# Chunk states of a state-space layer stored 576 instead of 512 bytes apart in SBUF

## The chip, the cores and the metric

The kernel runs on one core of a Trainium2 chip. The metric is device time in microseconds, the median of several executions.

## The reference, cut to what matters

Two branches are computed from the same `x` (2048 x 512) and mixed by a gate. One is softmax attention with 32 heads of 16 channels, the other a diagonal state-space convolution over 2048 steps with 512 channels.

```python
def _A_ref(x, wqkv, wo):                       # attention: 32 heads, Dh = 16
    scores = jnp.einsum("bhqd,bhkd->bhqk", q, k) * Dh ** -0.5
    p = _softmax(scores, axis=-1)              # 32 x 2048 x 2048 exponentials
    ...
def _B_ref(u, A_re, A_im, ...):                # state space, 128 states per channel
    K = jnp.einsum("dn,dnl,dn->dl", Cc, P, dB).real
    y = irfft(rfft(u) * rfft(K))               # causal convolution along time
    ...
return g * a + (1 - g) * b
```

The kernel computes the convolution in chunks of 64 steps. For each channel, a chunk leaves a complex state of 128 numbers (one per partition). A scan on VectorE carries the states from chunk to chunk, and the output of a chunk is a local product plus the carried state times a table.

Of the kernel before, what the change touches and what calls it, by code (L numbers as in the profile page):

```python
# [17 lines left out]
NCH = S // T  # L18
NBLK = 16
CB = D // NBLK  # L20
HALF_PI = math.pi / 2
NDSEM = 56

# [221 lines left out]
def declare(nc, es):  # L245
    B = {}

    def sb(name, free, dt=BF16):
        B[name] = Buf(name, "sb", free, dt)


    sb("KT", 4 * S)
    for k in range(4):
        sb(f"Q{k}", 4 * 512)
    sb("Qm", 2 * 512)
    sb("VE", 16 * 560)
    sb("ET", 7 * 1024)
    for k in range(4):
        sb(f"OnT{k}", S)
    sb("OT", 512, FP32)  # L260
    sb("ON", 512)
    sb("Rz", 2 * 16, FP32)
    sb("Wo", 4 * D)
    sb("xT", 4 * S)
    for n in ("Wk", "Wq", "Wv"):
        sb(n, 4 * D)
    sb("msk", 2, FP32)
    sb("piota", 4, FP32)
    sb("hpi", 1, FP32)

    sb("gwT", 4)
    sb("wm", D)
    sb("x0n", 4 * D)
    sb("idf", P, FP32)
    sb("idb", P)
    sb("gp", 16, FP32)
    sb("ge", 16, FP32)
    sb("g", 16, FP32)
    sb("g1", 16, FP32)
    sb("Dpb", 16)  # L280
    sb("Dp", 16, FP32)
    sb("Yl", 16 * D)
    sb("fo", 4 * D)

    for n in ("AreT", "AimT", "BreT", "BimT", "CreT", "CimT", "ldt", "dt"):
        sb(n, D)
    for n in ("an", "bn", "ba", "ea", "e2", "sb_", "cb", "u1", "u2", "u3", "u4", "zr", "zi"):
        sb(n, D, FP32)
    sb("wrb", D)
    sb("nwi", D)  # L290
    sb("VV", 2 * D, FP32)
    sb("VL", 2 * D, FP32)
    for n in ("L1", "L2", "L4", "L8", "L16", "L32", "L48"):
        sb(n, 2 * D, FP32)
    sb("MU", 3 * D, FP32)
    sb("pt1", 2 * D, FP32)
    sb("pt2", 2 * D, FP32)
    for n in ("D16", "D32", "D48"):
        sb(n, 2 * 2 * D)

    sb("FP", 2 * 128 * 8, FP32)
    sb("ft1", 2 * 64 * 8, FP32)
    sb("ft2", 2 * 64 * 8, FP32)
    for k in range(4):
        sb(f"B16{k}", 2 * 128 * 16)

    sb("PT", 2 * 2 * CB * T)
    sb("tt1", 2 * CB * 16)
    sb("tt2", 2 * CB * 16)
    sb("Qt", 2 * 32 * 128)  # L310
    sb("Sst", 4 * 512)
    sb("Kst", 2 * 8 * P)

    sb("SG0", 33 * 2 * 128)
    sb("SG1", 33 * 2 * 128)
    sb("G", 2 * 128, FP32)
    for n in ("s2", "s3"):
        sb(n, 2 * 128, FP32)

    sb("X2", 4 * 32 * 64)  # L320

    sb("Py", 3 * 2 * 16 * T)
    sb("Tt", 3 * 8 * 64)
    sb("Yst", 2 * 256)
    for i in range(3):
        B[f"SC{i}"] = Buf(f"SC{i}", "ps", 1024, FP32)
    B["OA"] = Buf("OA", "ps", 512, FP32)
    B["MB"] = Buf("MB", "ps", 512, FP32)
    for n, free in (("ptd", NBLK * P * 2 * CB * T), ("sd", D * NCH * 2 * P),
                    ("kpd", NBLK * P * 8 * P), ("xrd", S * D), ("ytd", D * S)):  # L330
        B[n] = Buf(n, "dr", free, BF16)
        B[n].t = nc.dram_tensor("gm_" + n, [free // P, P], BF16)
    for n in ("SC0", "SC1", "SC2", "OA", "MB"):
        B[n].t = es.enter_context(nc.psum_tensor(n, [P, B[n].free], FP32))
    for n in ("x", "w", "wo", "are", "aim", "bre", "bim", "cre", "cim", "ldt_d", "dsk_d", "gw_d", "out"):
        B["d_" + n] = Buf("d_" + n, "dr", 1, BF16)
    return B


def place(nc, bufs):  # L340

    base, end = (nc.sbuf_base + 31) // 32 * 32, nc.sbuf_usable_end
    sbs = [b for b in bufs.values() if b.kind == "sb" and b.first is not None]

    def fit(order):
        done, top = [], base
        for b in order:
            n = (b.nbytes() + 31) // 32 * 32
            busy = sorted((o.lo, o.hi) for o in done if o.first <= b.last + 1 and b.first <= o.last + 1)
            at = base  # L350
            for lo, hi in busy:
                if at + n <= lo:
                    break
                at = max(at, hi)
            b.lo, b.hi = at, at + n
            top = max(top, b.hi)
            done.append(b)
        return top

    best, seed = None, 1  # L360
    for k in range(400):
        def rank(b):
            nonlocal seed
            seed = (seed * 1103515245 + 12345) % 2 ** 31
            w = seed / 2 ** 31 * (0 if k < 2 else .8)
            return (-(b.last - b.first > 300) if k % 2 else 0, -b.nbytes() * (1 + w * 2) * (b.last - b.first + 20) ** (w if k >= 2 else 0))
        order = sorted(sbs, key=rank)
        top = fit(order)
        if best is None or top < best[0]:
            best = (top, order)  # L370
    assert best[0] <= end, (best[0] - end, live(sbs))
    fit(best[1])
    for b in sbs:
        b.over = [o for o in sbs if o is not b and o.lo < b.hi and b.lo < o.hi]
        b.order = b.first
        b.t = nc.alloc_sbuf_tensor_at(b.name, [P, b.free], b.dt, offset=b.lo)
    for b in bufs.values():
        if b.kind != "sb":
            b.over, b.order = (), 0
# [27 lines left out]
def record(nc, p, B, ins):  # L407
# [426 lines left out]
    def sload(blk):  # L834
        qr, bl = divmod(blk, 4)
        yield ("AFTER", f"S{blk}", 2)
        if qr >= 2:
            yield ("AFTER", f"yq{qr - 2}", 0)
        sg = SG[qr % 2]
        if bl == 0:  # L840
            op("POOL", lambda g: g.memset(sg(0, [[1, 256]]), 0.0), [], [(sg, "z")])
        dma("SP", lambda e: e.dma_start_transpose(sg(256 + CB * bl, [[128, 64], [1, CB]]),
                                                  sd.dram(CB * blk * 8192, [[8192, CB], [1, 8192]])),
            [(sd, (blk, i)) for i in range(4)], [(sg, bl, (qr, 'S'))])
        sch.mark(f"sg{blk}")


    def scan():
        G, s2, s3 = B["G"], B["s2"], B["s3"]
        MU = B["MU"]  # L850
        e = "DVE"

        def quarter(qr):
            sg, d0 = SG[qr % 2], 128 * qr
            ks = [(sg, bl, (qr, 'S')) for bl in range(4)]
            for bl in range(4):
                yield ("AFTER", f"sg{4 * qr + bl}", 12)
            for c in range(NCH - 1):
                so = 256 * (c + 1)
                if c == 0:  # L860
                    yield (e, .3)
                    op(e, lambda v, so=so: v.tensor_copy(G(0, [[1, 256]]), sg(so, [[1, 256]])), ks, [(G, 0)])
                    continue
                yield (e, .7)
                op(e, lambda v: v.tensor_tensor(s2(0, [[128, 2], [1, 128]]), G(0, [[128, 2], [1, 128]]),  # L865
                                                MU(d0, [[0, 2], [1, 128]]), ALU.mult), key("G", "MU"), [(s2, 0)])
                op(e, lambda v: v.tensor_tensor(s3(0, [[128, 2], [1, 128]]), G(128, [[-128, 2], [1, 128]]),  # L867
                                                MU(D + d0, [[D, 2], [1, 128]]), ALU.mult), key("G", "MU") + [(MU, 1)], [(s3, 0)])
                yield (e, .9)
                op(e, lambda v, so=so: v.tensor_tensor(s2(0, [[1, 256]]), s2(0, [[1, 256]]), sg(so, [[1, 256]]), ALU.add),  # L870
                   [(s2, 0)] + ks, [(s2, 0)])
                op(e, lambda v: v.tensor_tensor(G(0, [[1, 256]]), s2(0, [[1, 256]]), s3(0, [[1, 256]]), ALU.add),  # L872
                   [(s2, 0), (s3, 0)], [(G, 0)])
                op(e, lambda v, so=so: v.tensor_copy(sg(so, [[1, 256]]), G(0, [[1, 256]])), key("G"), ks)  # L874
            for bl in range(4):
                sg.tags[bl] = (qr, "G")
            sch.mark(f"scan{qr}")

        yield ("AFTER", "scanpar", 0)
        for qr in range(4):  # L880
            yield from quarter(qr)
# [20 lines left out]
    def ystage():  # L902
        def unit(u):
# [11 lines left out]
            for q in range(4):  # L915
# [7 lines left out]
                for ri in range(2):  # L923
                    for j in range(4):
                        i = 4 * q + j
                        mm(lambda q=q, j=j: MB(64 * q, [[1, 64]], 32 * j, 32),
                           lambda ri=ri, i=i: sg(ri * 128 + CB * bl + 16 * hf + i, [[256, 32]]),
                           lambda ri=ri, i=i: Py(r * YN + ri * 16 * T + i * T, [[1, T]]),
                           [(sg, b_, (qr, 'G')) for b_ in range(4)] + [(sg, "z"), (Py, r, u)], ky, False, ri == 1,
                           pos=(0, 32 * j))  # L930
# [241 lines left out]
```

## The kernel before: what the change touches

`SG0` and `SG1` hold the states of one quarter of the channels (128 channels), each in turn. A row of `SG` has 128 real parts, then 128 imaginary parts, as bf16. So the states of one channel in successive chunks lie 2 x 128 elements = 512 bytes apart.

```python
sb("SG0", 33 * 2 * 128)                 # 32 chunks and one row of zeros
sb("SG1", 33 * 2 * 128)
...
def sload(blk):                         # 16 blocks of 32 channels
    ...
    dma("SP", lambda e: e.dma_start_transpose(sg(256 + CB * bl, [[128, 64], [1, CB]]), ...
def quarter(qr):                        # the scan, on VectorE
    for c in range(NCH - 1):
        so = 256 * (c + 1)
        ...                             # s2 = G * MU_re ; s3 = swap(G) * MU_im
        op(e, lambda v, so=so: v.tensor_tensor(s2(0, [[1, 256]]), s2(0, [[1, 256]]), sg(so, [[1, 256]]), ALU.add), ...
        ...                             # G = s2 + s3
        op(e, lambda v, so=so: v.tensor_copy(sg(so, [[1, 256]]), G(0, [[1, 256]])), ...
def ystage():                           # the output: 32 units of 4 steps; one step is
    ...                                 # 4 matmuls MB<-Tt,X and these 8 matmuls MB<-Py,SG
        mm(lambda q=q, j=j: MB(64 * q, [[1, 64]], 32 * j, 32),
           lambda ri=ri, i=i: sg(ri * 128 + CB * bl + 16 * hf + i, [[256, 32]]),   # weights
           lambda ri=ri, i=i: Py(r * YN + ri * 16 * T + i * T, [[1, T]]), ...
```

The weights of such a matmul are 32 columns (one channel, 32 chunks), read with a step of 256 elements. `X`, the weight operand of the matmuls `MB<-Tt,X` and `MB<-Qt,X`, is read with a step of 64 elements (128 bytes).

Everything is recorded by a small scheduler in steps of one key tile `q` (0 to 511). In each step ScalarE runs two exponentials of 128x1024, TensorE runs the attention matmuls `SC<-Qm,KT` and `OA<-ET,VE`, and pieces of the state-space work are dealt out by a budget. All state-space matmuls write one PSUM tile, `MB`, so a piece must be evicted by VectorE before the next may start (in the kernel before, the matmuls `MB<-Qt,X` waited 22.1 us for this and `MB<-Tt,X` 8.4 us).

The softmax here doesn't subtract the row's maximum and nothing guards it: scores larger than these inputs give would overflow.

## Time and profile before

| what | value | where it is read |
|---|---|---|
| time | 1044.11 us (4 runs) | results |
| ScalarE busy | 978.2 us, 94% | page, part 1 |
| of it exponentials | 963.9 us in 1024 | page, part 5 |
| spacing of exponentials, undisturbed | 904 ns | records of the trace |
| the same beside `Py,SG` matmuls | 1078 ns | records of the trace |

In the views PE is TensorE's matmuls, PEld its weight loads, DVE is VectorE, ACT is ScalarE and POOL is GpSimd. The granted clock is the share of its full speed that TensorE was given. The page's first lines for the kernel before, with the busy time of each engine:

```profile
span 1040.5 us, 16316 instructions
...
PE 752.9 (72%) x6617; PEld 212.2 (20%) x6617; DVE 636.2 (61%) x1356; ACT 978.2 (94%) x1041; POOL 3.5 (0%) x11
```

ScalarE is the limit. At the undisturbed spacing its 1024 exponentials take 1023 x 0.904 = 925 us from the first start to the last. Where the rest goes is seen in the windows view of the kernel before. The columns are the stretch, then busy time and number of instructions on each engine, the granted TensorE clock, the DMA share and GB/s.

```profile
100.00:150.00 50.00, 36.68 (x266) 9.13 (x265) 41.19 (x58) 49.86 (x55) 0.00 (x0) 0.91 0.00 1
650.00:700.00 50.00, 42.63 (x484) 16.70 (x480) 6.39 (x14) 49.05 (x51) 0.31 (x1) 0.50 0.51 112
800.00:850.00 50.00, 41.80 (x480) 16.66 (x476) 43.41 (x113) 48.94 (x50) 0.00 (x0) 0.50 0.41 96
850.00:900.00 50.00, 43.90 (x496) 17.05 (x492) 4.31 (x11) 50.00 (x51) 0.00 (x0) 0.50 0.34 83
```

Read the fourth engine, ACT: from 850 to 900 us it is busy all of the time, but finishes 51 exponentials where it finished 55 in the earlier stretch. It is not waiting; each instruction takes longer. By the records, an exponential beside a `Py,SG` burst took 1256 ns (median) and the others of the output stage 1114 ns. In that stretch the output is computed. The timeline of the kernel before shows two of its steps (start, duration, engine, line, what, how many; idle time in brackets):

```profile
859.84 0.61 PE L420 MATMUL SC<-Qm,KT 32*128 32x512 bf16 x4 [0.18 <-ACT ET L537]
...
860.93 0.15 PEld L420 LDWEIGHTS MB<-Tt,X 64*32 64x32 bf16 x4 [0.44 <-issue]
860.93 0.28 PE L420 MATMUL MB<-Tt,X 64*32 64x64 bf16 x4
861.14 0.34 PEld L420 LDWEIGHTS MB<-Py,SG 128*32 128x32 bf16 x8
861.15 0.47 PE L420 MATMUL MB<-Py,SG 128*32 128x64 bf16 x8
861.79 0.11 PEld L420 LDWEIGHTS SC<-Qm,KT 32*128 32x128 bf16 x4 [0.31 <-ACT ET L537]
861.80 0.61 PE L420 MATMUL SC<-Qm,KT 32*128 32x512 bf16 x4 [0.18 <-ACT ET L537]
```

From one `SC` group to the next is 1.96 us for two exponentials. TensorE waits for ScalarE there (0.18 us), so TensorE is not the limit. The eight `Py,SG` weight loads take 0.34 us together.

The durations by tile in the kernel before (minimum, median, maximum in ns) compare the weight loads, and show a VectorE operation of the scan:

```profile
L420 PEld LDWEIGHTS MB<-Py,SG x1024: 162/226/279, 619.1 to 907.1; 128*32 128x32 bf16 x171
L420 PEld LDWEIGHTS MB<-Qt,X x512: 128/144/169, 247.7 to 617.5; 64*32 64x32 bf16 x171
L420 PEld LDWEIGHTS MB<-Tt,X x512: 128/137/141, 618.8 to 906.8; 64*32 64x32 bf16 x171
...
L870 DVE TENSOR_TENSOR s<-s,SG x120: 400/418/644, 334.3 to 841.5; 128x256 f32<-128x256 f32 x120
```

All load 32 columns. The step is 512 bytes for `SG` and 128 for `X`. The VectorE line has the same shape every time, yet ranges up to 644 ns: those are the ones that run beside `Py,SG` loads. In the records, all 51 multiplications and additions of the scan that took over 450 ns overlap such loads.

### The profile page before, as it was taken

Reading aid. Unit: us, or ns where it says so; the run is one execution under the profiler, and the core shown is the slowest. Engines: PE = TensorE matmul, PEld = TensorE weight load, DVE = VectorE, ACT = ScalarE, POOL = GpSimd, SP = SyncE. Lnnn points to the kernel's source line nnn. Section 1 sums busy time; section 2 is a strip of 40 time slices with the busy share of each in tenths; the row PEclk is TensorE's granted clock in tenths of the full one; section 3 lists DMA queues with packets and bytes.
Section 4 is the critical chain, followed back from the end, with each engine's and each line's share of the span. In section 5 each row is a group of like instructions: output and inputs, shape, how many; then the busy total and the mean of one; then the engine's idle time right before and its main releaser. Section 6 shows DMA issues by size and latency. Waiting matters only on the chain.

```text
span 1040.5 us, 16316 instructions
## 1 busy us (share of the span) xinstructions
PE 752.9 (72%) x6617; PEld 212.2 (20%) x6617; DVE 636.2 (61%) x1356; ACT 978.2 (94%) x1041; POOL 3.5 (0%) x11
## 2 busy tenths in 40 slices
PE   5867667666776656766577778888868888877765
PEld 2211112111111111111111123333313333311111
DVE  7737889996567997589876530116999951031201
ACT  5999999999999998999899989999999999999996
POOL 0000000000000000000000000000000000000000
PEclk8988987556665556655556665555555555557756
DMA  8700000007876007840057663465353434100000
GB/s 177 154 9 1 1 1 1 1 1 217 207 200 182 1 0 168 221 139 1 11 142 198 187 173 89 95 141 123 92 112 90 95 90 99 37 16 26 21 6 21
DMA packets 227404, 92.17 MB, mean 89 GB/s; under 512 B 191873, under 2 KB 215041, under 8 KB 225281
## 3 DMA queue, kind: packets, MB, share of 16 engines
q1 hardware_dynamic: 225600, 90.21, 34.7%
q10 hardware_dynamic: 1728, 0.92, 0.4%
q8 instruction: 52, 0.85, 0.3%
q14 instruction: 24, 0.19, 0.1%
HBM read 27.92 MB, written 35.65 MB: 61 GB/s over the span
## 4 chain that ended last, share of the span: by engine, by line
ACT 57%; DVE 27%; PE 12%; issue 2%; SPq 1%; DMA 1%; DVEq 0%; POOL 0%; POOLq 0%
ACT ET L537 56%; PE MB L420 6%; DVE G L872 4%; PE SC L420 4%; DVE s L870 4%; DVE s L867 3%; DVE s L865 3%; DVE SG L874 3%; PE OA L420 2%; DVE VE L503 1%; DVE OT L552 1%; SPq L896 1%; DVE VE L468 1%; DVE Sst L821 1%; DVE KT L510 1%
## 5 line engine op out<-in xcount | busy, mean ns | idle before, releaser
L537 ACT ACTIVATE ET<-SC 128x1024 bf16<-128x1024 f32 x1024 | 963.9, 1110 | 40.0 <-PE SC L420 39.0
L420 PE MATMUL SC<-Qm,KT 32*128 32x512 bf16 x2048 | 288.4, 554 | 212.6 <-ACT ET L537 207.5
L420 PE MATMUL OA<-ET,VE 128*32 128x512 bf16 x2048 | 286.0, 562 | 0.1
L420 PEld LDWEIGHTS SC<-Qm,KT 32*128 32x128 bf16 x2048 | 54.6, 97 | 411.3 <-ACT ET L537 396.4
L420 PEld LDWEIGHTS OA<-ET,VE 128*32 128x32 bf16 x2048 | 53.7, 101 | 188.6 <-issue 183.6
L932 DVE CAST Yst<-MB 128x256 bf16<-128x256 f32 x32 | 13.4, 418 | 117.9 <-PE MB L420 117.9
L552 DVE STREAM_TRANSPOSE OT<-OA 128x512 f32<-128x512 f32 x32 | 24.0, 751 | 73.8 <-PE OA L420 73.6
L821 DVE CAST Sst<-MB 128x256 bf16<-128x256 f32 x64 | 27.0, 422 | 62.4 <-PE MB L420 55.0
L562 DVE TENSOR_TENSOR tt<-B,D 128x1024 bf16<-128x1024 bf16 x96 | 62.0, 687 | 1.3
L420 PE MATMUL MB<-Py,SG 128*32 128x64 bf16 x1024 | 59.8, 314 | 1.2 <-issue 1.2
L420 PE MATMUL MB<-Qt,X 64*32 64x256 bf16 x512 | 39.3, 398 | 27.2 <-DVE Sst L823 22.1
L872 DVE TENSOR_TENSOR G<-s,s 128x256 f32<-128x256 f32 x120 | 54.3, 452 | 4.1
L870 DVE TENSOR_TENSOR s<-s,SG 128x256 f32<-128x256 f32 x120 | 53.5, 446 | 0.0
L867 DVE TENSOR_TENSOR s<-G,MU 128x256 f32<-128x256 f32 x120 | 52.7, 439 | 0.0
L865 DVE TENSOR_TENSOR s<-G,MU 128x256 f32<-128x256 f32 x120 | 50.7, 422 | 0.1
L420 PEld LDWEIGHTS MB<-Py,SG 128*32 128x32 bf16 x1024 | 42.8, 222 | 9.2 <-issue 1.3
L1021 DVE SCALAR_TENSOR_TENSOR fo<-MB,g,Yl 128x512 bf16<-128x512 f32 x13 | 9.7, 747 | 55.2 <-PE MB L420 55.2
L420 PE MATMUL MB<-Tt,X 64*32 64x64 bf16 x512 | 35.7, 268 | 8.5 <-DVE Yst L932 8.4
L874 DVE CAST SG<-G 128x256 bf16<-128x256 f32 x120 | 35.5, 295 | 4.1
L562 DVE TENSOR_TENSOR PT<-tt,tt 128x1024 bf16<-128x1024 bf16 x48 | 33.2, 692 | 1.6
L562 DVE TENSOR_TENSOR ft<-FP,L 128x1024 f32<-128x1024 f32 (+1 forms) x32 | 33.7, 1085 | 0.4
L420 PEld LDWEIGHTS MB<-Tt,X 64*32 64x32 bf16 x512 | 19.0, 136 | 63.1 <-issue 62.8
(115 smaller groups left out, 415.7 us busy)
## 6 DMA issues: line engine op xcount, KB each, us to landing
gm_ptd<-PT SPq DMA_DIRECT2D x16, 1024.0 KB, 5.0
Py<-gm_ptd SPq DMA_DIRECT2D x32, 512.0 KB, 4.4
gm_sd<-Sst SPq DMA_DIRECT2D x64, 128.0 KB, 2.3
gm_kpd<-Kst SPq DMA_DIRECT2D x16, 256.0 KB, 3.5
Tt<-gm_kpd SPq DMA_DIRECT2D x128, 32.0 KB, 3.4
gm_xrd<-in_A_x_dram SPq DMA_DIRECT2D x1, 2048.0 KB, 13.1
X<-gm_xrd SPq DMA_DIRECT2D x8, 256.0 KB, 4.7
gm_ytd<-Yst SPq DMA_DIRECT2D x32, 64.0 KB, 1.8
```

What stands on the lines that cost most here:

```text
L420: op("PE", lambda t: t.matmul(out(), lhsT(), rhs(), start=start, stop=stop, skip_group_check=True, **kw), R, W)
L468: op("DVE", lambda v: v.memset(VE(0, [[1, 16 * 560]]), 1.0), [], [(VE, k) for k in range(16)])
L537: op("ACT", lambda a: a.activation(ET(1024 * e, [[1, 1024]]), sc(0, [[1, 1024]]), AF.Exp, scale=DH ** -0.5), [(sc, 0, h // 2), (sc, 1, h / ...
L552: op("DVE", lambda v: v.transpose(OT(o, [[1, 512]]), OA(0, [[1, 512]])), [(OA, 0, b)], [(OT, 0, b)])
L562: op(eng, lambda v: v.tensor_tensor(o(), a(), b_(), f), R, W)
L821: op("DVE", lambda v, bank=bank: v.tensor_copy(Sst(512 * bank, [[256, 2], [1, 128]]), MB(0, [[256, 2], [1, 128]])), [(MB, 0, ('S', blk, ba ...
L865: op(e, lambda v: v.tensor_tensor(s2(0, [[128, 2], [1, 128]]), G(0, [[128, 2], [1, 128]]), MU(d0, [[0, 2], [1, 128]]), ALU.mult), key("G", ...
L867: op(e, lambda v: v.tensor_tensor(s3(0, [[128, 2], [1, 128]]), G(128, [[-128, 2], [1, 128]]), MU(D + d0, [[D, 2], [1, 128]]), ALU.mult), k ...
L870: op(e, lambda v, so=so: v.tensor_tensor(s2(0, [[1, 256]]), s2(0, [[1, 256]]), sg(so, [[1, 256]]), ALU.add), [(s2, 0)] + ks, [(s2, 0)])
L872: op(e, lambda v: v.tensor_tensor(G(0, [[1, 256]]), s2(0, [[1, 256]]), s3(0, [[1, 256]]), ALU.add), [(s2, 0), (s3, 0)], [(G, 0)])
L874: op(e, lambda v, so=so: v.tensor_copy(sg(so, [[1, 256]]), G(0, [[1, 256]])), key("G"), ks)
L932: op("DVE", lambda v: v.tensor_copy(Yst(r2 * 256, [[1, 256]]), MB(0, [[1, 256]])), ky, [(Yst, r2, u)])
```

## The change

The intent: a row of a part becomes 144 elements instead of 128, so that columns lie 576 bytes apart instead of 512. The larger buffers need room, so the first use of `SG1` is held back until a later table block is written, and the search for addresses gets a second phase (left out below).

```diff
+RS = 144
-    sb("SG0", 33 * 2 * 128)
-    sb("SG1", 33 * 2 * 128)
+    sb("SG0", 33 * 2 * RS)
+    sb("SG1", 33 * 2 * RS)
 ...
         if qr >= 2:
             yield ("AFTER", f"yq{qr - 2}", 0)
+        elif qr == 1:
+            yield ("AFTER", "pt11", 4)
 ...
-        dma("SP", lambda e: e.dma_start_transpose(sg(256 + CB * bl, [[128, 64], [1, CB]]),
+        dma("SP", lambda e: e.dma_start_transpose(sg(2 * RS + CB * bl, [[RS, 64], [1, CB]]),
 ...
-                so = 256 * (c + 1)
+                so = 2 * RS * (c + 1)
 ...                                     # scan: [[1, 256]] on SG becomes [[RS, 2], [1, 128]]
-                           lambda ri=ri, i=i: sg(ri * 128 + CB * bl + 16 * hf + i, [[256, 32]]),
+                           lambda ri=ri, i=i: sg(ri * RS + CB * bl + 16 * hf + i, [[2 * RS, 32]]),
```

The hold moves work in the recorded order. The second quarter's scan starts about 12 to 16 key tiles later, and some state matmuls move with it.

More of the change, by code (lines that the diff above doesn't have):

```diff
@@ L369, in place @@
         if best is None or top < best[0]:
+            best = (top, order)
+    for k in range(3000):
+        if best[0] <= end:
+            break
+        order = list(best[1])
+        seed = (seed * 1103515245 + 12345) % 2 ** 31
+        i = seed % len(order)
+        seed = (seed * 1103515245 + 12345) % 2 ** 31
+        j = (seed >> 8) % len(order)
+        order.insert(j, order.pop(i))
+        top = fit(order)
+        if top <= best[0]:
             best = (top, order)
@@ L838, in sload @@
             yield ("AFTER", f"yq{qr - 2}", 0)
+        elif qr == 1:
+            yield ("AFTER", "pt11", 4)
         sg = SG[qr % 2]
         if bl == 0:
-            op("POOL", lambda g: g.memset(sg(0, [[1, 256]]), 0.0), [], [(sg, "z")])
-        dma("SP", lambda e: e.dma_start_transpose(sg(256 + CB * bl, [[128, 64], [1, CB]]),
+            op("POOL", lambda g: g.memset(sg(0, [[1, 2 * RS]]), 0.0), [], [(sg, "z")])
+        dma("SP", lambda e: e.dma_start_transpose(sg(2 * RS + CB * bl, [[RS, 64], [1, CB]]),
                                                   sd.dram(CB * blk * 8192, [[8192, CB], [1, 8192]])),
@@ L858, in quarter @@
             for c in range(NCH - 1):
-                so = 256 * (c + 1)
+                so = 2 * RS * (c + 1)
                 if c == 0:
                     yield (e, .3)
-                    op(e, lambda v, so=so: v.tensor_copy(G(0, [[1, 256]]), sg(so, [[1, 256]])), ks, [(G, 0)])
+                    op(e, lambda v, so=so: v.tensor_copy(G(0, [[128, 2], [1, 128]]), sg(so, [[RS, 2], [1, 128]])), ks, [(G, 0)])
                     continue
@@ L869, in quarter @@
                 yield (e, .9)
-                op(e, lambda v, so=so: v.tensor_tensor(s2(0, [[1, 256]]), s2(0, [[1, 256]]), sg(so, [[1, 256]]), ALU.add),
+                op(e, lambda v, so=so: v.tensor_tensor(s2(0, [[128, 2], [1, 128]]), s2(0, [[128, 2], [1, 128]]), sg(so, [[RS, 2], [1, 128]]), ALU.add),
                    [(s2, 0)] + ks, [(s2, 0)])
@@ L873, in quarter @@
                    [(s2, 0), (s3, 0)], [(G, 0)])
-                op(e, lambda v, so=so: v.tensor_copy(sg(so, [[1, 256]]), G(0, [[1, 256]])), key("G"), ks)
+                op(e, lambda v, so=so: v.tensor_copy(sg(so, [[RS, 2], [1, 128]]), G(0, [[128, 2], [1, 128]])), key("G"), ks)
             for bl in range(4):
```

## The prediction

> **What bounds the kernel now.** ScalarE. Page part 1: ACT is busy 978.2 of 1040.5 us (94%); 963.9 us of it is 1024 exponentials of 128x1024. Individual records start 904 ns apart when nothing disturbs them: 1023 x 0.904 = 925 us. The rest is 20 us before the first, 10 us after the last, and about 84 us of excess in between. The windows view shows where: 54 or 55 exponentials per 50 us in undisturbed stretches, only 50 or 51 from 600 to 900 us, where the state-space output is computed.
>
> **Why that stretch is slow.** An exponential beside the Py,SG matmuls is followed 1078 ns later (median of 111) by the next, instead of 918 ns at the same granted clock (0.5). Exponentials beside Qt,X loads (39, 920 ns) or Tt,X loads alone (4, 917 ns) are not slowed. All three write the same PSUM bank; the weight load differs: X columns lie 128 bytes apart, SG columns 512. By groups, SG loads take 222 ns for 32 columns, X loads 136 to 146, contiguous VE loads 101. VectorE operations overlapping SG loads stretch too (s<-s,SG 418 to 608 ns). [...]
>
> **What the change does.** Columns now lie 576 bytes apart, an odd multiple of 64. No operation is added or removed; the scan's accesses become two runs of 128 (same element counts, about equal time, off the critical path), the zero fill grows to 288 columns. Larger buffers need room, so the second quarter's state loads are held back, the second scan starts some 12 to 16 key tiles later, and buffers may get other addresses. The instruction order shows state matmuls moving there and the output stage ending three key tiles later; nothing at the very end moves.
>
> **Cost on the critical path.**
> - 128 bursts of 8 SG loads (334 ns each): at most 128 x (1078 - 918) = 20.5 us. X at 128 bytes costs none; with a residual of 25 ns the gain is 17 us.
> - The collision of the second scan's end with state matmuls (at 513.8 us: 3.7, then 1.4 us) disappears; one double step is added (1.4 to 2 us): gain 3 us.
> - Output-stage stalls with two steps in one tile stay about equal in number (8 us in all), slightly shorter: 0.5 us.
> - Waits for state stores at 603 and 610 us (1.7, 2.1 us): unchanged.
>
> Sum 20.5 us; 1043.5 - 20.5 = **1023 us**, range 1016 to 1035. Faster by over 2%: 0.48; within 2%: 0.50; slower: 0.02.
>
> **What would show it.** Right: SG loads near 130 to 150 ns; no step above 950 ns between exponentials beside them; 53 or 54 exponentials per 50 us from 650 to 900; no scan operation near 600 ns; the stall after the second scan gone. Wrong: loads short but exponentials still 1078 ns (then it is PSUM or the matmuls); loads still 222 ns (then 576 collides too).
>
> **What would make it wrong.** [...] new addresses causing conflicts elsewhere; new stalls from the moved scan or from stores queued behind loads; the clock granted at other places.

What it calls a PSUM bank is the tile `MB`, which the trace names as the output of all three groups. The sum: 17 + 3 + 0.5 = 20.5 us. The residual of 25 ns was a guess of mine, read from no trace; with the spacings read from the trace it gives 128 x (1078 - 918 - 25) = 17 us. That the scan would take about equal time with two runs of 128 was an estimate too; the medians of its additions `s<-s,SG` were 418 ns before and after.

## The result, and the profile after

The time fell from 1044.11 to 1027.16 us (4 runs each; the prediction had three of the runs of before, with a median of 1043.52; 1026.37 to 1028.83 after). The ratio is 0.9841, 95% interval 0.9823 to 0.9859. A ratio is the mean time of one kernel's runs over that of the other's of the same rounds, so it is not quite the ratio of the medians. The gain is clear of the noise, but by the limit of 2% that this study uses the verdict is "same". In later rounds, on the chip of the second set of experiments, the changed kernel was run again and the ratio was 0.9803 (0.9782 to 0.9823), an interval that reaches across 2%.

The page of the kernel after:

```profile
span 1027.0 us, 16317 instructions
...
PE 740.6 (72%) x6617; PEld 195.9 (19%) x6617; DVE 626.7 (61%) x1356; ACT 959.0 (93%) x1041; POOL 3.6 (0%) x11
```

The same stretches in the windows view of the kernel after:

```profile
100.00:150.00 50.00, 36.69 (x265) 9.14 (x265) 40.00 (x54) 48.81 (x54) 0.00 (x0) 0.90 0.00 1
650.00:700.00 50.00, 43.73 (x532) 15.15 (x528) 6.31 (x14) 50.00 (x55) 0.34 (x1) 0.50 0.47 108
800.00:850.00 50.00, 42.26 (x500) 14.20 (x496) 39.72 (x113) 49.38 (x55) 0.00 (x0) 0.50 0.41 97
850.00:900.00 50.00, 43.50 (x528) 14.96 (x524) 6.58 (x15) 50.00 (x56) 0.00 (x0) 0.50 0.34 79
```

ACT now finishes 54 to 56 exponentials per 50 us in the output stage (54 in the two stretches from 700 to 800 us, not shown), as many as in the undisturbed stretch, at the same granted clock of 0.50. An exponential beside a burst took 1129 ns, against 1256 before. The corresponding steps in the timeline of the kernel after:

```profile
859.73 0.61 PE L433 MATMUL SC<-Qm,KT 32*128 32x512 bf16 x4 [0.18 <-ACT ET L550]
...
861.03 0.21 PEld L433 LDWEIGHTS MB<-Py,SG 128*32 128x32 bf16 x8
861.03 0.34 PE L433 MATMUL MB<-Py,SG 128*32 128x64 bf16 x8
861.55 0.11 PEld L433 LDWEIGHTS SC<-Qm,KT 32*128 32x128 bf16 x4 [0.32 <-ACT ET L550]
861.56 0.61 PE L433 MATMUL SC<-Qm,KT 32*128 32x512 bf16 x4 [0.19 <-ACT ET L550]
```

The step is 1.83 us instead of 1.96, and the eight loads take 0.21 us instead of 0.34. TensorE waits for ScalarE as long as before (0.18 and 0.19 us), so the gain came through ScalarE's own pace, not through TensorE's shorter work. By tile:

```profile
L433 PEld LDWEIGHTS MB<-Py,SG x1024: 132/150/178, 633.8 to 901.4; 128*32 128x32 bf16 x171
...
L885 DVE TENSOR_TENSOR s<-s,SG x120: 410/418/422, 338.9 to 839.9; 128x256 f32<-128x256 f32 x120
```

The loads fell to 150 ns, and the scan is not stretched any more: this operation took 422 ns at most (644 before), and the longest of the scan's multiplications and additions 427 ns (653 before).

To find where the time went, I took the start of each exponential from the records and added up what its distance to the next exceeds 904 ns. The stretches are given by the number of the exponential (0 to 1023), so that both kernels are compared at the same place of the attention work. The last column also has the time after the last exponential's start.

| us of excess | start, 0 to 231 | states 231 to 447 | 447 to 533 | 533 to 613 | output 613 to 905 | 905 to end |
|---|---|---|---|---|---|---|
| before | 17.1 | 14.5 | 7.4 | 9.0 | 30.5 | 17.3 |
| after | 21.2 | 15.0 | 3.4 | 14.7 | 9.2 | 18.7 |
| difference | +4.1 | +0.5 | -4.0 | +5.7 | **-21.3** | +1.5 |

The sum is -13.5 us, the difference of the two profiled spans. The medians differ by more, 16.95 us: the profiled run of the changed kernel was the slowest of its four. The output stage gained more than expected. The state stage from 447 to 613 lost 1.7 us where a gain of 3 us was expected. The start lost 4.1 us. I take most of this for scatter between executions, because the clock was granted at other moments: from 13 to 30 us it was 0.89 before and 0.66 after, and the fourth exponential was followed by the next after 1.90 and 3.96 us. Over all ten traces the start lies between 17.1 us (clock 0.89 in that stretch) and 21.7 us (0.55), and a kernel that differs from the one before only in the layout of `SG` had 19.5. A small cost of the new addresses is not excluded: the two kernels with the old ones had 17.1 and 19.5 us, the eight with new ones 18.7 to 21.7.

The cut at exponential 613 is a compromise. The first `Py,SG` burst stands at exponential 610 before and at 616 after, and a stall of 2.0 us at exponential 613 of the kernel after lies between its last state matmuls. Cut at each kernel's own first burst, the stretch from 447 went from 15.8 to 20.1 us, a loss of 4.3, and the output stage from 31.0 to 7.2 us, a gain of 23.8.

### The profile page after: what moved, and what is told of

It reads as the page before. It is cut to its first block, busy times and chain, and to the rows that moved or that the text cites. A ratio compares the mean times of both kernels' runs of the same rounds, so it can differ in the third digit from the quotient of the medians.

```text
span 1027.0 us, 16317 instructions
## 1 busy us (share of the span) xinstructions
PE 740.6 (72%) x6617; PEld 195.9 (19%) x6617; DVE 626.7 (61%) x1356; ACT 959.0 (93%) x1041; POOL 3.6 (0%) x11
## 4 chain that ended last, share of the span: by engine, by line
ACT 61%; DVE 21%; PE 12%; SPq 3%; issue 2%; DMA 1%; DVEq 0%; POOL 0%; POOLq 0%
ACT ET L550 60%; PE MB L433 6%; PE SC L433 4%; DVE G L887 3%; PE OA L433 2%; DVE s L885 2%; DVE s L882 2%; DVE s L880 2%; DVE SG L889 2%; DMA gm_sd<-Sst 1%; SPq L787 1%; DVE VE L516 1%; DVE OT L565 1%; DVE VE L481 1%; SPq L911 1%
## 5 line engine op out<-in xcount | busy, mean ns | idle before, releaser
L550 ACT ACTIVATE ET<-SC 128x1024 bf16<-128x1024 f32 x1024 | 944.8, 1097 | 44.7 <-PE SC L433 43.7
L947 DVE CAST Yst<-MB 128x256 bf16<-128x256 f32 x32 | 13.5, 421 | 116.1 <-PE MB L433 116.1
L887 DVE TENSOR_TENSOR G<-s,s 128x256 f32<-128x256 f32 x120 | 51.0, 425 | 4.1
L880 DVE TENSOR_TENSOR s<-G,MU 128x256 f32<-128x256 f32 x120 | 50.1, 417 | 0.1
L882 DVE TENSOR_TENSOR s<-G,MU 128x256 f32<-128x256 f32 x120 | 50.1, 418 | 0.0
L885 DVE TENSOR_TENSOR s<-s,SG 128x256 f32<-128x256 f32 x120 | 50.1, 418 | 0.0
L433 PE MATMUL MB<-Py,SG 128*32 128x64 bf16 x1024 | 44.3, 260 | 1.4 <-issue 1.4
L810 DVE CAST Kst<-MB 128x512 bf16<-128x512 f32 x16 | 11.0, 689 | 36.9 <-PE MB L433 36.9
L433 PE MATMUL MB<-xT,Wk 128*128 128x512 bf16 x64 | 22.5, 440 | 15.2 <-DVE xT L1078 8.0
```

What stands on the lines that cost most here:

```text
L433: op("PE", lambda t: t.matmul(out(), lhsT(), rhs(), start=start, stop=stop, skip_group_check=True, **kw), R, W)
L550: op("ACT", lambda a: a.activation(ET(1024 * e, [[1, 1024]]), sc(0, [[1, 1024]]), AF.Exp, scale=DH ** -0.5), [(sc, 0, h // 2), (sc, 1, h / ...
L810: op("DVE", lambda v: v.tensor_copy(Kst(1024 * (blk % 2) + 63, [[P, 8], [1, T]]), MB(0, [[T, 8], [1, T]])), [(MB, 0, ('K', blk)), (Kst, "z ...
L880: op(e, lambda v: v.tensor_tensor(s2(0, [[128, 2], [1, 128]]), G(0, [[128, 2], [1, 128]]), MU(d0, [[0, 2], [1, 128]]), ALU.mult), key("G", ...
L882: op(e, lambda v: v.tensor_tensor(s3(0, [[128, 2], [1, 128]]), G(128, [[-128, 2], [1, 128]]), MU(D + d0, [[D, 2], [1, 128]]), ALU.mult), k ...
L885: op(e, lambda v, so=so: v.tensor_tensor(s2(0, [[128, 2], [1, 128]]), s2(0, [[128, 2], [1, 128]]), sg(so, [[RS, 2], [1, 128]]), ALU.add), ...
```

## The experiments

Eight kernels were run, four on each of two chips. In the tables "burst" is the time from the start of the first to the end of the last of the eight `Py,SG` loads of a step, and "spacing" is the distance from the exponential that runs beside a burst to the next one. Both are medians over the bursts. By this count the kernel before has 334 and 1083 ns, the kernel after 213 and 921 ns (128 bursts each).

Theory: the step at which the weight loads read SBUF decides how long ScalarE's and VectorE's instructions take beside them; the moved order is a separate, small cost. Rivals: new addresses or the moved order made the gain; or the way in which states are written did; or TensorE's shorter bursts did.

### Undo the step alone

```diff
-RS = 144
+RS = 128
+RA = 144
-    sb("SG0", 33 * 2 * RS)                 # SG1 likewise
+    sb("SG0", 33 * 2 * RA)
```

Addresses, sizes and the recorded order stay those of the changed kernel. Only the columns are 512 bytes apart again.

> The changed kernel with its buffers, addresses and instruction order, but the states again 512 bytes apart inside the larger buffer. Theory (the step of the loads): SG loads back to about 222 ns, bursts of 334 ns, 1078 ns between exponentials beside them, output stage about 20 us longer than after, total 1045 to 1049 us. Rival (new addresses or the moved schedule made the gain): total stays near 1027 us and the exponentials at about 921 ns.

Measured: 1048.54 us, ratio to the kernel before 1.0019 (0.9983 to 1.0054), result correct. By tile in this run:

```profile
L434 PEld LDWEIGHTS MB<-Py,SG x1024: 149/225/284, 634.3 to 923.5; 128*32 128x32 bf16 x171
...
L886 DVE TENSOR_TENSOR s<-s,SG x120: 402/419/634, 338.7 to 856.9; 128x256 f32<-128x256 f32 x120
```

The burst was 334 ns and the spacing 1087 ns. The output stage had 30.9 us of excess, against 9.2 after. All of the gain is gone although addresses and order are the new ones, and the scan is stretched again. That rules out the first rival.

### Only the reading with 512 bytes

```diff
-   sg(ri * RS + CB * bl + 16 * hf + i, [[2 * RS, 32]])
+   sg(ri * RS + CB * bl + 16 * hf + i, [[256, 32]])     # wrong data on purpose
```

The states are written as in the changed kernel. The unused columns of each row are zeroed first, so that no unwritten byte is read.

> Wrong result on purpose: the states are written 576 bytes apart as in the changed kernel, only the weight loads read with a step of 512 bytes (wrong data, same count; the pad columns are zeroed so that nothing unwritten is read). Theory (reading alone): loads near 222 ns, exponentials beside them at about 1078 ns, about 1047 us. Rival (the way states are written, by the transposing transfer or by VectorE): loads near 150 ns, 921 ns, about 1027 us.

Measured: 1039.66 us (one run, state unknown), wrong result as intended. By tile in this run:

```profile
L433 PEld LDWEIGHTS MB<-Py,SG x1024: 151/206/275, 632.6 to 914.8; 128*32 128x32 bf16 x171
```

Burst 316 ns, spacing 1023 ns, output stage 23.8 us. Reading alone brings back about 15 of the 21 us, so the writing is not the main cause. But the spacing falls short of the expected 1078 ns. In what is read, one thing differs from the kernel before besides the data: the real and the imaginary part of a channel lie 288 bytes apart here and 256 there. This was taken up in the last experiment.

### Sweeps of the step

```diff
+STEPS = [1, 32, 64, 128, 192, 256, 264, 288]          # second run: [256, 258, 260, 264, 268, 272, 280, 288]
-   sg(ri * RS + CB * bl + 16 * hf + i, [[2 * RS, 32]])
+   sg(ri * RS + CB * bl + 16 * hf + i, [[STEPS[u % 8], 32]])   # wrong data on purpose
```

Each of 32 output units uses one of eight steps, so a single run gives 16 bursts of each. The unused columns are zeroed here too, as in every run with wrong data.

> Wrong result on purpose: the changed kernel, but the load step differs by output unit (unit mod 8): 2, 64, 128, 256, 384, 512, 528, 576 bytes. Theory [...]: the burst and the following exponential are worst at 512 (334 ns, 1078 ns), between at 256, and free (921 ns) at 2, 64, 128, 528 and 576; 384 behaves like 128. Rival [...]: every step from 64 on behaves alike.

> Wrong result on purpose, as the sweep before with steps 512, 516, 520, 528, 536, 544, 560, 576 bytes. Theory [...]: 516 nearly as bad as 512, 520 and 528 between, 544 to 576 free. Rival (only an exact multiple of 512 collides): 516 is as free as 576.

Measured (1029.24 and 1028.52 us, one run each, state unknown, wrong results as intended):

| step, bytes | remainder by 256 | burst, ns | spacing, ns |
|---|---|---|---|
| 2 | contiguous | 139 | 904 |
| 64 | 64 | 213 | 921 |
| 128 | 128 | 264 | 921 |
| 256 | 0 | 314 | 1037 |
| 384 | 128 | 267 | 921 |
| 512 | 0 | 314 / 314 | 1030 / 1054 |
| 516 | 4 | 231 | 920 |
| 520 | 8 | 222 | 920 |
| 528 | 16 | 207 / 207 | 921 / 920 |
| 536 | 24 | 204 | 920 |
| 544 | 32 | 210 | 920 |
| 560 | 48 | 221 | 920 |
| 576 | 64 | 214 / 214 | 921 / 920 |

In the steps tried, the burst goes with the remainder of the step by 256: 64 and 576 agree (213 and 214 ns), 128 and 384 agree (264 and 267 ns), 256 and 512 agree (314 ns). Two expectations failed. A step of 256 bytes is as bad as one of 512 (spacing 1037 ns, against 1030 and 1054) and not in between. And 516 bytes, expected to be nearly as bad as 512, leave ScalarE undisturbed (920 ns), as the rival of the fine sweep had said; that only exact multiples of 512 would be bad did not hold, since 256 is as bad. The rival "every step alike" also falls. Of the steps tried, only 256 and 512 slow the exponentials (1030 to 1054 ns, all others 904 to 921). The steps of 128 and 384 bytes lengthen TensorE's loads (264 and 267 ns) but leave ScalarE alone (921 ns). Each step always falls on the same place in a row of `SG`, but place cannot explain this: in the kernel before the medians of all eight places lie between 1054 and 1118 ns. One thing the sweeps leave open: no burst of any run took between 277 and 303 ns, and all shorter ones left ScalarE near 920 ns or less. So a limit by the length of the burst would fit as well as one by the remainder.

### A layout without padding: 128 bytes

If a step of 128 bytes is good enough for ScalarE (921 ns in the sweep), no padding is needed. The states can be stored block by block: for each of four blocks of 32 channels, the rows of 32 real and 32 imaginary parts follow each other, so columns lie 128 bytes apart and `SG` keeps its old size.

```diff
 # against the kernel before
+SB_ = 33 * 2 * CB
-   e.dma_start_transpose(sg(256 + CB * bl, [[128, 64], [1, CB]]), ...
+   e.dma_start_transpose(sg(SB_ * bl + 2 * CB, [[CB, 64], [1, CB]]), ...
-   sg(so, [[1, 256]])                                  # scan, so = 256 * (c + 1)
+   sg(so, [[CB, 2], [SB_, 4], [1, CB]])                # scan, so = 2 * CB * (c + 1)
-   sg(ri * 128 + CB * bl + 16 * hf + i, [[256, 32]])
+   sg(SB_ * bl + ri * CB + 16 * hf + i, [[2 * CB, 32]])
```

> The kernel before with the states laid out block by block (run of 32 channels, real and imaginary part side by side), so that columns lie 128 bytes apart; no byte of padding, no hold, buffers at the addresses of before and the same instruction order on every engine. Theory (step decides, and the moved plan is a separate cost): bursts about 264 ns, exponentials beside them 921 ns, the output stage about 20 us shorter than before, 1022 to 1025 us, a little faster than the changed kernel. Rival (bursts must become as short as 213 ns for the gain): output stage only half as much shorter, about 1034 us.

Measured: 1024.04 us, ratio 0.9792 (0.9771 to 0.9814), correct. The windows view of this run in the output stage, and its loads by tile:

```profile
650.00:700.00 50.00, 44.19 (x524) 16.24 (x520) 6.79 (x16) 48.90 (x55) 0.31 (x1) 0.50 0.60 124
850.00:900.00 50.00, 42.54 (x472) 14.29 (x468) 10.75 (x31) 50.00 (x55) 0.00 (x0) 0.50 0.26 60
```

```profile
L421 PEld LDWEIGHTS MB<-Py,SG x1024: 138/173/220, 621.0 to 888.9; 128*32 128x32 bf16 x171
...
L871 DVE TENSOR_TENSOR s<-s,SG x120: 415/418/423, 336.7 to 828.3; 128x256 f32<-128x256 f32 x120
```

The bursts took 261 ns, clearly longer than with 576 bytes, and yet the spacing was 920 ns, the scan was not stretched, and ScalarE ran 55 exponentials per 50 us in these stretches (53 or 54 in the three between). The output stage had 11.0 us of excess. So the gain does not need bursts as short as 213 ns: the last rival falls. The order and the addresses are those of the kernel before, so this is also the cleanest measure of the layout alone, though the distance between the two parts changed with it, from 256 to 64 bytes. That it would be a little faster than the changed kernel did not show: the intervals overlap.

### 576 bytes without the hold

```diff
 # against the changed kernel
-        elif qr == 1:
-            yield ("AFTER", "pt11", 4)
-    sb("SG0", 33 * 2 * RS)                  # SG1 likewise
+    sb("SG0", 32 * 2 * RS)                  # the last chunk's state is never read
-   sg(2 * RS + CB * bl, [[RS, 64], [1, CB]])
+   sg(2 * RS + CB * bl, [[RS, 62], [1, CB]])
-    sb("Rz", 2 * 16, FP32)
+    sb("Rz", 16, FP32)                      # one half serves both heads
```

Two simpler ways to this, rows of 140 and of 136 elements, did not build.

> The changed kernel with 576 bytes but the instruction order of before: the hold of the second quarter is gone, room is made by not loading the last chunk's state, which nobody reads, and by sharing one small tile. Theory (the moved plan cost the missing microseconds): bursts 213 ns, 921 ns, state stage between exponentials 447 and 613 like before (about 16 us of excess instead of 18), total 1021 to 1025 us, 2 to 4 us below the changed kernel. Rival (the plan is neutral): equal to the changed kernel, 1027 us.

> The changed kernel itself, as the reference for the other runs of this chip: 1027 us, ratio to before 0.984. Theory and rival agree.

Measured on the same chip in the same rounds: without the hold 1025.70 us, ratio 0.9801 (0.9780 to 0.9823); the changed kernel again 1025.96 us, ratio 0.9803 (0.9782 to 0.9823). Both correct, and equal within the interval. The expected 2 to 4 us did not show in the time.

| us of excess | 0 to 231 | 231 to 447 | 447 to 533 | 533 to 613 | 613 to 905 | 905 to end |
|---|---|---|---|---|---|---|
| before | 17.1 | 14.5 | 7.4 | 9.0 | 30.5 | 17.3 |
| after (first profile) | 21.2 | 15.0 | 3.4 | 14.7 | 9.2 | 18.7 |
| change again | 20.3 | 15.2 | 3.6 | 14.9 | 9.5 | 15.9 |
| 576, no hold | 21.7 | 15.1 | 7.4 | 8.7 | 10.4 | 16.7 |
| 128, no padding | 19.5 | 14.5 | 7.4 | 7.8 | 11.0 | 17.3 |
| new plan, 512 | 20.9 | 15.2 | 3.6 | 15.0 | 30.9 | 16.5 |

From 447 to 613 the three kernels with the new plan have 18.1 to 18.6 us and the three with the old one 15.2 to 16.4 us. So the moved plan does cost about 2.5 us there, but it gives about 1 us back in the output stage (9.2 and 9.5 against 10.4 at 576 bytes), and the rest is within the scatter of the other columns. Cut at each kernel's first burst, both effects are larger: up to it 16.1 us without the hold and 20.8 for the change again, in the output stage 10.4 and 7.2 us. So the moved plan costs nearly 5 us before the output and gives about 3 us back in it.

### The distance between the two parts

```diff
+OFFS = [128, 144, 64, 32, 16, 8, 256, 136]
-   sg(ri * RS + CB * bl + 16 * hf + i, [[2 * RS, 32]])
+   sg(ri * OFFS[u % 8] + CB * bl + 16 * hf + i, [[256, 32]])   # wrong data on purpose
```

> Wrong result on purpose: load step 512 bytes everywhere, but the imaginary part starts 256, 288, 128, 64, 32, 16, 512 or 272 bytes after the real part (by unit mod 8). In the read-only run both parts lay 288 bytes apart and cost 1023 ns instead of 1083. Theory [...]: 256 and 512 give bursts of 334 ns and about 1083 ns, all others about 315 and 1023 ns. Rival (how the states are written explains the difference): all offsets alike, about 315 and 1023 ns.

Measured (1040.03 us, one run, state unknown, wrong result as intended):

| distance, bytes | 256 | 512 | 288 | 128 | 64 | 32 | 16 | 272 |
|---|---|---|---|---|---|---|---|---|
| burst, ns | 334 | 335 | 312 | 313 | 316 | 314 | 317 | 318 |
| spacing, ns | 1109 | 1070 | 986 | 1013 | 1061 | 1050 | 968 | 1021 |

The bursts came as expected: 334 and 335 ns at 256 and 512 bytes, 312 to 318 elsewhere, so the rival (all alike) falls for them, and the shorter bursts of the read-only run (316 ns at a distance of 288 bytes) agree with the 312 ns at 288 here. The spacing does not settle as much. 256 and 512 bytes are highest (1109 and 1070 ns), but 64 and 32 bytes come close to them (1061 and 1050), where about 1023 was expected. Each distance also falls on one place in a row (unit modulo 8), and place alone moves the spacing: in the read-only run, where the distance is 288 bytes everywhere, the medians of the eight places run from 968 to 1084 ns. At the place where this sweep gave 1109 ns with 256 bytes, the read-only run had 1084 ns. So the shortfall of the read-only run in spacing is only in part explained.

## Why the prediction was right, point by point

- **What bounds the kernel and why the output stage is slow: right.** The loads' step was named as what differs (128 bytes for `X`, 512 for `SG`), and the experiments isolate it: same addresses and order with 512 bytes give back 1048.54 us.
- **Loads "near 130 to 150 ns": right** (150). "No step above 950 ns between exponentials beside them": the median is 921 ns; single steps above that remain (7 of 124); in the four longest ScalarE itself sat idle before the next exponential. "53 or 54 exponentials per 50 us": 54 to 56. "No scan operation near 600 ns": right, 427 at most.
- **The size of the main term was too small.** "With a residual of 25 ns the gain is 17 us" was mis-sized: no residual is left (921 against 918 to 921 ns undisturbed at this clock). Of the 21.3 us that the output stage gained, about 19 us is spacing: the exponentials beside bursts that are in no stall exceeded 904 ns by 21.3 us together before and by 2.0 after. Its stalls of over 0.5 us also shrank by about 2 us (8.0 to 5.9, added up from the records), where 0.5 us had been expected; without the one at exponential 613, which belongs to the state stage, they fell to 3.9 us.
- **The step that failed:** "The collision of the second scan's end with state matmuls disappears; one double step is added: gain 3 us." (A double step is a key tile with two pieces of state-space work.) The collision left its old place (-4.0 us), but its like came up elsewhere: +5.7 us from exponential 533 to 613, or 7.7 us up to 616, where the output of the kernel after begins. In the kernel before the eviction of a state matmul queued behind the scan on VectorE; in the kernel after it queues behind the table's operations. The timeline of the kernel before:

```profile
515.62 0.42 DVE L872 TENSOR_TENSOR G<-s,s 128x256 f32<-128x256 f32 x1
516.08 0.29 DVE L874 CAST SG<-G 128x256 bf16<-128x256 f32 x1
516.29 0.41 DVE L821 CAST Sst<-MB 128x256 bf16<-128x256 f32 x1
516.62 0.41 DVE L823 TENSOR_SCALAR Sst<-MB 128x256 bf16<-128x256 f32 x1
...
517.18 0.65 PE L420 MATMUL MB<-Qt,X 64*32 64x256 bf16 x8 [3.75 <-DVE Sst L823]
```

and of the kernel after, 35 us further on:

```profile
550.26 1.29 DVE L575 TENSOR_TENSOR tt<-B,D 128x1024 bf16<-128x1024 bf16 x2
551.59 0.69 DVE L575 TENSOR_TENSOR PT<-tt,tt 128x1024 bf16<-128x1024 bf16 x1
552.20 0.42 DVE L834 CAST Sst<-MB 128x256 bf16<-128x256 f32 x1
552.53 0.41 DVE L836 TENSOR_SCALAR Sst<-MB 128x256 bf16<-128x256 f32 x1
...
553.00 0.66 PE L433 MATMUL MB<-Qt,X 64*32 64x256 bf16 x8 [2.80 <-DVE Sst L836]
...
561.16 0.42 DVE L834 CAST Sst<-MB 128x256 bf16<-128x256 f32 x1 [1.63 <-DMA gm_sd<-Sst]
561.97 0.66 PE L433 MATMUL MB<-Qt,X 64*32 64x256 bf16 x8 [2.78 <-DVE Sst L836]
```

- The number in the brackets of the MATMUL lines is TensorE's idle time: 3.75 us once before; 2.80 us and, behind a state store, 2.78 us after. I had counted double steps in the instruction order, but not what VectorE had in its queue at the new place, and had taken the waits for state stores as unchanged.
- **Luck in the sum.** 1027 us came near the predicted 1023 partly because two misses cancel: the main term was about 4 us too small (17 against 21.3), and the second about 5 us too good (a gain of 3 against a loss of 1.7).
- **The mechanism in the memory: not shown.** My reading of it was a guess: the sweeps show which of the steps tried are slow, and no run shows what in the memory makes them so. What the experiments show is that the step of PE's weight reads decides how long ScalarE's and VectorE's instructions take beside them: the spacing was 1083 ns with 512 bytes, 921 with 576 and 920 with 128, and the addition `s<-s,SG` took up to 644, 422 and 423 ns. The stretched operations of the scan have all their operands in SBUF. An exponential reads PSUM and writes `ET` in SBUF, and no run separates the two, so which of them takes longer is not shown. Nor did ScalarE wait for TensorE: in the kernel before it sat idle after only 5 of the 124 exponentials beside a burst.

## What to carry to other kernels

When an engine's instruction takes longer without waiting for anything, look at what the other engines read beside it: here each burst of eight weight loads with a step of 512 bytes on TensorE cost ScalarE about 160 ns (a spacing of 1083 ns, against 921 with 576 bytes), and TensorE itself was not the limit. Of the steps tried, 256 and 512 bytes were the ones to avoid (1030 to 1054 ns in the sweeps); 516 instead of 512 was enough (920 ns), and rearranging the data gave the same gain as padding it (ratios 0.9792 and 0.9803), without the memory or the moved order. When padding forces the order of work to move, a stall that leaves one place may come back in another (here -4.0 and +5.7 us), so look at each engine's queue at the new place and not at the old place alone.
